# A hand-scheduled attention and two-MLP kernel: the written order of all steps is replaced by another order

## The chip, the cores and the metric

The kernel runs on one core of a Trainium2 chip. The metric is the device time of one execution in microseconds (us), as a median of several runs. Smaller is better.

## The reference

Three stages follow each other.

- Attention for 4 batches and 8 heads, with 576 positions and head size 64: scores are scaled, every score below the row's maximum minus tau is masked out, softmax is taken over the rest, and the result multiplies V.
- The first MLP on 2304 tokens of width 512: `h = x @ w_in` (512 to 2048), then a rational function of h elementwise (`g = P(h) / (Q(h) + 1e-6)`, a cubic over a quadratic in |h|), then `g @ w_out` back to 512.
- The second MLP: `a = x @ w1`, `b = x @ w2` (both 512 to 1024), `h = a * b @ w3`, and `h @ w_out2` to 512 columns.

Inputs and outputs are float32; the weights come as 64-bit floating point words.

## The kernel before

**Precision and weights.** Products that need it are made with a value split into a high and a low float16 part, three matrix products for one. The weights arrive as 64-bit words, 512 KB for a tile of 128 rows and 512 columns. `raw_w` (L670) loads one such tile into one of three buffers `wr`; `conv_w` turns it into a 32-bit tile `cw` in two steps (a cast on a chosen engine, L336 or L340, and a combination on VectorE, L681); `split_w` makes the high and low parts, partly with a small matrix product (L733, L734). `w_product` (L930) multiplies w3 by w_out2 once, so that the second MLP has one product less for each token. `norm_w` (L697) is a matrix product that sums squares of weights.

**Attention.** For each batch b, pair of heads c and block of 128 rows: `load_qk` and `load_v` fetch inputs; `scale_q` (L338 or L342) scales q by a factor that depends on tau (`limits`, L408 to L411, loads tau and makes this `flag`); `qk` (L507, L512) makes scores in the two banks `S` of PSUM; `top` (L521) takes row maxima; `thr`, `exp` (L541 to L548), `recip`, `p_norm`, `p_hi`, `p_lo` make normalized probabilities split in two; `p_t` (L584) transposes them by DMA into `pT`; `pv` (L599) multiplies by V; `x_split` and `x_tail` store the result in two parts `xp` and `xl`.

**MLPs.** The 18 token tiles n go through `h_product` (L809) for four chunks f, `act_h` (L817 to L824, ScalarE), `num` (L829, L831, VectorE, which ends the use of the bank of h), `den`, `inv`, `quotient` (L848 to L852 and a product L352), `turn` (L861, a transposing DMA from `gg` to `gt`) and `y_product` (L873). `y_norm`, `y_split` and another `turn` lead to the second MLP: `ab_product` (L980), `a_copy`, `c_mul` (L992 and two more), `turn`, `o_product` (L1009), `o_store` (L1021, L1025).

**PSUM.** There are two banks each (with places 0 and 1) of the tags `S`, `h` and `y`; `S` tiles are two banks wide. `h_product`, `pv`, `norm_w`, `w_product`, `scale_f` and most `ab_product` share the two places of `h`, so each must wait until the last reader of the place's former content is done.

**What sets the order.** All work is a list of 2533 events, numbered from 0. A text, `ORDER`, lists 3944 steps: each token is an event's number, and an event that has several steps stands several times. A letter behind the number says on which engine the step's free choice falls: `a` ScalarE, `v` VectorE, `p` GpSimd. Figures behind dots say which buffer or bank of a tag each new tile takes, in the order in which the step asks for tiles. The program is issued in exactly this order, so each engine, and SyncE (which issues all DMAs), works through its own steps in this order and waits at each for its inputs and for its buffer. Nothing else in the file decides the order. The events that the prediction speaks of are 1 (`limits`), 0 (`setup`: memsets on GpSimd, table load on ScalarE), 14 and 15 (`load_qk` and `scale_q` of the first q), 23 and 51 (the first two `qk`), 28, 36, 48 and 52 (`raw_w`), 30, 50 and 54 (`conv_w`), 56 (the first `w_product`), 80 (the first `pv`), 358 (`pv` of batch 0, pair 0, rows 256 to 511), 459, 478 and 527 (`h_product` of tile 0, chunks 1 and 2, and of tile 1, chunk 0), 2502 and 2503 (`o_product` and `o_store` of tile 15), 2531 and 2532 (the last `o_product` and `o_store` of tile 17).

The loop that issues the steps is this:

```
for token in ORDER.split():
    token, *where = token.split(".")
    places[:] = map(int, where)
    n = int(token.rstrip("apv"))
    eng[0] = token[len(str(n)):]
    if n not in gens:
        fn, args, *_ = events[n]
        gens[n] = fn(*args)
    if gens[n] is not None:
        next(gens[n], None)
```

Of the kernel before, what the change touches and what calls it, by code (L numbers as in the profile page):

```python
# [32 lines left out]
52.0 48.1 14.0.1 0 54p.0 54.0 50v.1 28.2 50.1 36.0 1 15a 23.0.1 30p.0 3 30.2 44.1 8.0 6.1 4.2  # L33
38a.1 10.2 25.0 27 29v.0 31.0.2 31v 33.3 33v 51.0.1 19.4.5 5.0.0 9.1 46p.0 46.3 7.0 35p 16.1 35
37p 45v.6 38.4 11.1 47 53.1 55 57v.1 59.1.7 62.8 21v 86.0.1 59a 12 12.0 12 18a.0 84v.0.0 84 32.0
13a.1.1 62a 64p 90.0.1 49.0 18.5 20.1 64 74a.3 13 76 92.2 24.2 88a 34v.1 39p.6 41p 94 22v.0
17a.2.2 22.6 96a.2 98.2.8 100.2 56.1 34.7 100a 17 66a 2 78 98a 102p 40.1 26v.0 43.1 119.0.1 26.8
68p.3 121.3 123 70p 56 102 113v.4 125a.0 115 127.3.5 61.0 63v.1 63.9 42v.0 42.10 127a 72 154.7.6
129.2 80.0.0 129a 158.1.0 131p 131 65.2 133v 82v 67v.1 103.0 104a 107p.3 82 109v 56 69.0 141a.8
160.0 56 69 162 117.0 75.1 105v.0 143 111.1 145 164p.1 105.11 166.4.4 168.2 166v 77p.0 67.12 168v  # L40
170v 116.0 186.1.0 77.13 106.2 135a.3 69 137v 170 172v 174p.8 188.1 152a.3.3 152 156a 190 176v
118p.1 69 58a.14 71a.15 79.1 118.16 192v.2 195.5.5 195a 139 81v.0 83.1 73.0 81.17 180v.0 83 182
108p.1 197.1 197a 108.18 147.0 199v 120.0 621.1 223.1.0 149a 149 132.2 122v.0 122.19 89.0 178.2
225.2 110.0 199 83 227 229p.0 231.6.4 231a 233.3 83 233a 235a 85a.20 91p.1 134v.0 110 134.21 136.1
201v 91.22 203p.2 205p 209a.8 211 184.0 252.1.0 110 110 97.1 624v.0 97 624.23 171.2 93.0 207 647.1
254.3 256 235 237a 258p.1 246a.0 260.7.6 260a 95v.1 95.24 97 97 248 641.0 219.7.5 650v.0 650.25
173p.1 262.1 645a.0 645.26 262a 221a 288 112v.27 124.1 290.1.0 291.0 264a 173.28 240a.2 652.0 242p
652 126v.0 163.0 264 126.29 274a.3 99a.30 213 266p 148.2 165a.1 293 150p.0 295a.2 165.31 140.1
150.32 652 628.0 297.0.4 276 613.1 298.8 298a 613 630p.1 297a 142v.0 314.0.1 142.33 316.1 300a
87.0 318 319a.0 613 300 321.1.1 321a 309v.5 128.0 630.34 250.1 613 616a.35 339.0 302v 304p.0 210.2  # L50
268p.7 212p.0 179.1 181a.1 278 155.0 311 284.8.3 286p 212.36 218.2 181.37 305v 633.1 220p.1 341.2
633 633 157a.0 633 157.38 342v.1 323.4 187.1 636v.39 270v 323a 652 655v.40 215.1 220.41 217a 217
130.0 60.0 159.0 138 194.0 167.1 161.1 226.2 196a.0 325v 169 175.0 344.2.6 189v.1 189.42 234.1 177
196.43 228v.1 144.1 325 146 183.0 228.44 202.0 185 185 151.1 241.2 153 153 312.0 191.0 193.1
204v.0 236p.1 344a 367.1.0 236.45 244.2 198.1 346v 327.1 346 659.0 114.0 200 204.46 230.0 243v.1
243.47 369.3 370 222.1 272 285.0 224.0 365 214.1 232 206.0 208 238.0 216 216 245.1 372a.2 239 326v
# [12 lines left out]
428v 380.0 407p 409 470p 470 478.0 357v.0 478 289.0 480.0 484.0.1 471p 480.0 661.1 480.0 392p.1
324.1 361.2 345.1 485p 482 479a.4 486.3 488 482 458 392.34 487 487 490p.0 454.0 491.7.8 690.0  # L70
493.3 472v 474p.2 491a 481 394.1 527.0 364a.1 661 357.3 359.1 724.1 489.0 493a 414 338.1 693p.0
364.10 366.1 678v.25 310.1 489 439.2 495a 509.0 511.0 396 281.0 281a 283.1 283a 396.1 396 424v.21
427v.41 455.1.0 401a.32 496.1 489 512a.1 527 406v.33 495 672v.29 417v.31 476p 514.0.7 399v.1 489v
514a 496 456p 417.0 516p 401.1 529.1 693.37 529.1 529.1 413a.38 534p 430.6 540.1.0 727p.1 492.1
499.0 440.1.0 499.0 417v 497a 401a 531 431v.28 408v.43 413.0 403a.42 531 432.0 498a.5 542.1 544
676v.46 546p.2 433v 403.1 413v 536 516 775.0 424.0 500p 403a 431.1 777v.0 473.2 501 420a.44 433
536 777.36 504a.6 477.1 434v.45 431a 727.47 499.0 503p 424a 547.1.8 549.2 435.0 549a 547a 505
664p.0 437a 506 422v.6 518a 434.1 501 427.0 712.2 545.1 434v 672.1 506 502 538.0 538 545 538 538v
695.1 442.0 672v 408.1 686a.12 415v.22 437 483.0 427v 698.0 701.1 551v 704p.0 507 410a.26 565.0.1
704.3 519v.3 436a.23 422.0 567.2 539 521p 569 444.1 570p.0 408a 449.1 429v.11 715a.1 715.10 415.1  # L80
# [1159 lines left out]
```

## Time and profile before

| | |
|---|---|
| median of three runs | 1026.38 us (1025.14 to 1026.40) |
| profiled execution, its own time | 1025.45 us |
| its span, first to last instruction | 1023.6 us |
| TensorE (PE) busy | 961.6 us, 94% |
| VectorE (DVE) busy | 799.8 us, 78% |
| ScalarE (ACT) busy | 673.8 us, 66% |
| GpSimd (POOL) busy | 337.0 us, 33% |
| mean granted clock of TensorE, share of full | 0.986 |

The own time of the profiled execution is 1.85 us more than its span: what lies around the first and the last instruction. Busy shares are means over the whole span; the rows further down tell them for stretches of it. SPq is SyncE's sequencer, which issues the DMAs.

### The profile page before, as it was taken

To read this page: it belongs to the slowest core of one execution; us is meant where nothing else is said; L and a number is where in the kernel's file an instruction comes from. 1 tells how busy PE (TensorE), PEld (TensorE's weight loads), DVE (VectorE), ACT (ScalarE), POOL (GpSimd) and SP (SyncE) were. 2 spreads that over 40 slices of the span, in tenths; PEclk is the share of its full clock that TensorE was granted. 3 is DMA by queue.
4 is the path that set the end of the run, shared out by engine and by line. 5 is a ranking of instruction groups with operands and counts; after the bars stand their busy time and mean duration, and the time that the engine had idled before them with its cause. 6 is when DMAs were issued, how large, how long until landed. Compare 5 with 4: busy or idle time off the path is not lost. (4 is left out here: it accounts for less than half of the span.)

```text
span 1023.6 us, 15533 instructions
## 1 busy us (share of the span) xinstructions
PE 961.6 (94%) x5260; PEld 459.4 (45%) x5260; DVE 799.8 (78%) x1529; ACT 673.8 (66%) x1262; POOL 337.0 (33%) x374
## 2 busy tenths in 40 slices
PE   2899787999899999999999999999999999999998
PEld 1344243444444444554545454544444444444443
DVE  5775699989798888998778788998888667676721
ACT  4546689998768897678667777787656435544411
POOL 2223134343233343532334333343233222233220
PEclk9999798999999999999999999999999999999999
DMA  8999879978857687957765685677664455333233
GB/s 285 230 235 251 244 211 216 212 200 194 187 124 147 140 150 169 201 130 151 148 135 117 135 181 115 151 134 150 125 130 91 97 107 104 70 60 69 60 58 76
DMA packets 334047, 153.32 MB, mean 150 GB/s; under 512 B 307344, under 2 KB 311440, under 8 KB 333968
## 3 DMA queue, kind: packets, MB, share of 16 engines
q1 hardware_dynamic: 333968, 152.34, 67.5%
q8 instruction: 41, 0.67, 0.3%
q14 instruction: 38, 0.31, 0.1%
HBM read 68.67 MB, written 8.13 MB: 75 GB/s over the span
## 5 line engine op out<-in xcount | busy, mean ns | idle before, releaser
L873 PE MATMUL y<-wp,gt 128*128 128x512 f16 x864 | 199.1, 379 | 0.7 <-DMA gt<-gg 0.5
L809 PE MATMUL h<-wp,xp 128*128 128x512 f16 x768 | 181.1, 384 | 11.5 <-DVE U L831 5.8
L980 PE MATMUL h<-wp,yy 128*128 128x512 f16 x576 | 131.7, 379 | 3.1 <-DMA yy<-d_y 1.2
L873 PEld LDWEIGHTS <-gt 128*128 128x128 f16 x864 | 82.7, 98 | 104.8 <-issue 7.1
L809 PEld LDWEIGHTS <-xp 128*128 128x128 f16 x768 | 74.3, 99 | 105.6 <-issue 17.4
L521 DVE TENSOR_REDUCE m<-S 128x1 f32<-128x576 f32 x144 | 103.8, 747 | 16.9 <-PE S L512 11.0
L352 POOL TENSOR_TENSOR gg<-A,r 128x512 f16<-128x512 f32 x45 | 61.5, 1368 | 161.2 <-DVE A L852 80.1
L512 PE MATMUL S<-raw 64*128 64x288 f32 x512 | 90.3, 452 | 21.5 <-ACT raw L338 14.1
L543 ACT ACTIVATE S<-S,th 128x576 f32<-128x576 f32 x125 | 86.8, 708 | 31.2 <-POOL th L359 15.8
L1009 PE MATMUL y<-wp,gt 128*128 128x512 f16 x432 | 101.0, 379 | 0.0
L548 ACT ACTIVATE p<-S,xy 128x576 f32<-128x576 f32 x125 | 92.3, 740 | 10.1 <-DVE hl L352 2.9
L980 PEld LDWEIGHTS <-yy 128*128 128x128 f16 x624 | 59.9, 98 | 79.1 <-issue 8.2
L352 POOL TENSOR_TENSOR A<-A,r 128x512 f32<-128x512 f32 x47 | 61.8, 1315 | 86.3 <-ACT r L824 81.4
L352 POOL TENSOR_TENSOR hl<-p,hl 128x576 f16<-128x576 f32 x50 | 66.8, 1337 | 58.1 <-ACT hl L336 28.2
L817 ACT ACTIVATE U<-h,cf 128x512 f32<-128x512 f32 x72 | 55.7, 774 | 42.7 <-PE h L809 34.0
L512 PEld LDWEIGHTS S<-raw 64*128 64x128 f32 x512 | 50.0, 196 | 59.0 <-issue 16.0
L848 DVE SCALAR_TENSOR_TENSOR gg<-U,cf,r 128x512 f16<-128x512 f32 x72 | 55.9, 777 | 25.7 <-ACT r L841 17.4
L839 ACT ACTIVATE r<-A,lnb 128x512 f32<-128x512 f32 x72 | 51.7, 718 | 36.8 <-POOL A L352 19.0
L829 DVE SCALAR_TENSOR_TENSOR U<-h,cf,U 128x512 f32<-128x512 f32 x72 | 53.5, 744 | 23.4 <-ACT U L817 12.6
L681 DVE SCALAR_TENSOR_TENSOR cw<-rw,head 128x512 int32<-128x512 int32 x72 | 51.8, 725 | 17.8 <-POOL head L340 10.7
L1009 PEld LDWEIGHTS <-gt 128*128 128x128 f16 x432 | 41.4, 98 | 51.1 <-issue 2.7
L349 DVE SCALAR_TENSOR_TENSOR hl<-p,su,hl 128x576 f16<-128x576 f32 x64 | 58.6, 919 | 4.5 <-ACT hl L338 4.1
(202 smaller groups left out, 1648.3 us busy)
## 6 DMA issues: line engine op xcount, KB each, us to landing
rw<-in_moe_w_dram SPq DMA_DIRECT2D x32, 511.8 KB, 4.4
rw<-in_moe_w_out_dram SPq DMA_DIRECT2D x24, 511.8 KB, 4.9
raw<-in_k_dram SPq DMA_DIRECT2D x32, 288.0 KB, 3.4
rw<-in_moe_w_in_dram SPq DMA_DIRECT2D x16, 511.8 KB, 5.0
wr<-in_v_dram SPq DMA_DIRECT2D x13, 576.0 KB, 4.6
out_dram<-A SPq DMA_DIRECT2D x16, 256.0 KB, 2.3
wr<-in_v_dram SPq DMA_DIRECT2D x12, 320.0 KB, 3.5
d_y<-x SPq DMA_DIRECT2D x13, 256.0 KB, 2.3
```

The lines of the kernel that those rows point to most:

```text
L349: nc.vector.scalar_tensor_tensor(o, x, scale, hi, op0=ALU.mult, op1=ALU.subtract)
L352: (nc.gpsimd if eng[0] == "p" else nc.vector).tensor_tensor(o, x, y, op=op)
L512: nc.tensor.matmul(t[s][:, half, :HS], x[r, o:o + 128], y[r, keys], start=True, stop=True)
L521: nc.vector.tensor_reduce(st["m", b, c, blk][:, s:s + 1], t[:, :, :HS], axis=AX.XY, op=ALU.max, negate=True)
L543: nc.scalar.activation(t, t, AF.Prelu, bias=th, alpha=BIG)
L548: nc.scalar.activation(x, t, AF.Exp, bias=xy[:, 0:1], accum_out=su)
L809: nc.tensor.matmul(t, x[:, y, c, o:o + 128], w[:, a, :], start=c + i == 0, stop=c == KD - 1 and i == 2)
L817: nc.scalar.activation(u, h, AF.Identity, bias=cf[:, 15:16], scale=cf[:, 0:1])
L848: stt(p[:, 0, :], u, cf[:, 3:4], r, ALU.add, ALU.mult)
L873: nc.tensor.matmul(st["y", n], x[:, 4 * a + j, :], w[:, y, :], start=f + j + i == 0, stop=f == 3 and j == 3 and i == 2)
L980: nc.tensor.matmul(t, x[:, 4 * y + c, :], w[:, a, :], start=c + i == 0, stop=c == KD - 1 and i == 2)
L1009: nc.tensor.matmul(st["o", n], x[:, 4 * a + j, :], w[:, y, :], start=hf + j + i == 0, stop=hf == 1 and j == 3 and i == 2)
```

## The change

`ORDER` is replaced by another list of the same 3944 steps of the same events. No function changes. The new order was found by a search that drew durations of VectorE, GpSimd and of landing transfers at random around their medians; the old one was found with the medians alone. Steps have moved by 8 places in the median; 148 stand at the same place. 580 steps run on another engine than before; the letters in all are `a` 479, `v` 379, `p` 323 before, and 496, 389 and 296 after. Many tiles take another buffer. The diff replaces all 250 lines; these are the ones around the steps named above.

```
-52.0 48.1 14.0.1 0 54p.0 54.0 50v.1 28.2 50.1 36.0 1 15a 23.0.1 30p.0 3 30.2 44.1 8.0 6.1 4.2
-38a.1 10.2 25.0 27 29v.0 31.0.2 31v 33.3 33v 51.0.1 19.4.5 5.0.0 9.1 46p.0 46.3 7.0 35p 16.1 35
...
-129.2 80.0.0 129a 158.1.0 131p 131 65.2 133v 82v 67v.1 103.0 104a 107p.3 82 109v 56 69.0 141a.8
...
-275v.19 332 350.5 450 416.0 459.1 445 387.1 381p.1 459 358.1.0 418.1 375.1 419a.1 421.5.8 421a
...
-428v 380.0 407p 409 470p 470 478.0 357v.0 478 289.0 480.0 484.0.1 471p 480.0 661.1 480.0 392p.1
...
-493.3 472v 474p.2 491a 481 394.1 527.0 364a.1 661 357.3 359.1 724.1 489.0 493a 414 338.1 693p.0
...
-2524.2 2496.0 2528a.0 2529 2496 2529p.1 2502 2525.1 2529v 2525 2530.0 2531 2531 2532a.1 2532 2502
-2503v.0 2503
...
+28.0 14.0.1 1 15p 52.1 8.0 0 30v.0 30.0 54v.1 23.0.1 25.0 36.2 27 54.1 29a.0 31.0.2 33.3 31v 33v
+35v 35 48.0 45v.4 50a.0 38p.1 38.2 47 4.1 5.0.0 50.3 9.1 51.0.1 3 10.1 11.0 53.1 55 6.2 7.1 57a.1
...
+42.8 26.9 72 75.2 119.0.1 56.1 113a.0 80.0.0 17 115 121.3 63a.1 65.1 104a 107v.4 109p 123 63.10
...
+441 267a 263.1 281v.24 363v 294a.0 294.22 87.1 387.0 347.1 261a 398v 358.1.1 402p 443.0 350v.1
...
+418.1 419p.1 421.6.7 421a 336.14 390.2 338.0 368.1 275v.19 269.1 452.0 360 273v.6 459.0 375.0
...
+308v.0 428p 467.5.4 471 308.23 354.1 478.0 471 471v 343.2 469.1 478 467a 331.1 469a 279a.5 484.0.1
...
+396 676a.20 669a.30 409 511.0 489 512p.1 493a 454.1 527.1 439.2 514.7.6 396.0 281a 474v.5 283v 396
...
+2521 2526.1 2526 2500v.1 2495.1 2527 2500p 2522v.0 2523 2523a.0 2523v 2496.1 2482.0 2482 2527 2488
+2488 2447 2501.0 2528a.1 2524.2 2529 2529v.1 2496 2489a.0 2502 2489 2529p 2519 2530.1 2502 2503a.1
+2525.0 2503 2525 2531 2531 2532a.0 2532
```

## Rows read from the trace of the kernel before

**Rows 1.** Busy time of each engine in stretches (instructions in brackets), TensorE's granted clock, DMA share

```profile
0.00:61.20 61.20, 37.52 (x118) 17.46 (x118) 41.12 (x89) 30.66 (x59) 16.92 (x29) 1.00 0.91 254
61.20:102.00 40.80, 38.43 (x135) 18.05 (x136) 26.34 (x46) 21.50 (x46) 11.54 (x14) 1.00 0.99 243
102.00:205.00 103.00, 84.16 (x402) 38.16 (x400) 89.64 (x183) 88.60 (x185) 35.10 (x39) 0.87 0.89 221
205.00:1000.00 795.00, 782.38 (x4520) 377.25 (x4521) 638.55 (x1208) 530.39 (x971) 272.83 (x293) 1.00 0.63 130
1000.00:1023.60 23.60, 19.13 (x89) 8.48 (x87) 4.17 (x6) 2.69 (x4) 0.61 (x1) 0.98 0.26 61
```

**Rows 2.** What TensorE waited for, 0 to 102: us in total, times, longest

```profile
PE S L512 <- ACT raw L338: 14.1, 2, 12.2
...
PE h L599 <- DMA pT<-hl: 2.0, 2, 1.7
PE h L930 <- DVE cw L681: 1.4, 1, 1.4
```

**Rows 3.** What TensorE waited for, 102 to 205

```profile
PE h L697 <- ACT sq L688: 4.6, 7, 1.3
PE h L809 <- DVE U L831: 4.5, 1, 4.5
PE h L809 <- DVE xp L349: 3.2, 1, 3.2
```

**Rows 4.** What TensorE waited for, 205 to 1000, longest and shortest of 17 rows

```profile
PE h L809 <- DVE xp L349: 1.5, 1, 1.5
...
PE h L809 <- DVE xl L349: 0.2, 1, 0.2
```

**Rows 5.** Timeline of all engines, 0 to 13: start, us, engine, line, operation, idle before

```profile
1.64 0.43 SPq L451 DMA_DIRECT2D raw<-in_q_dram  x1
...
2.59 3.64 SPq L670 DMA_DIRECT2D rw<-in_moe_w_out_dram  x2
4.38 0.76 POOL L340 CAST head<-rw 128x512 f16<-128x512 bf16 x1 [2.48 <-DMA rw<-in_moe_w_dram]
...
5.78 0.45 DVE L340 CAST head<-rw 128x512 f16<-128x512 bf16 x1
6.26 0.43 SPq L408 DMA_DIRECT2D tau_t<-in_tau_dram  x1
...
11.46 0.15 DVE L409 TENSOR_SCALAR flag<-tau_t 128x1 f32<-128x1 f32 x1 [4.50 <-DMA tau_t<-in_tau_dram]
```

**Rows 6.** Groups of instructions by shape: count, busy us, mean ns, idle before

```profile
L342 POOL TENSOR_SCALAR raw<-raw,flag 128x256 f32<-128x256 f32 x1 | 1.4, 1450 | 0.0
```

**Rows 7.** Timeline of TensorE, 10 to 64

```profile
29.75 2.07 PE L930 MATMUL h<-cw 128*128 128x512 f32 x2
...
42.38 1.17 PE L599 MATMUL h<-pT,vh 128*64 128x256 f16 x18 [1.68 <-DMA pT<-hl]
...
45.20 7.33 PE L930 MATMUL h<-cw 128*128 128x512 f32 x16
```

**Rows 8.** Timeline of TensorE, 95 to 210

```profile
142.75 2.75 PE L809 MATMUL h<-wp,xp 128*128 128x512 f16 x12
...
165.35 4.45 PE L809 MATMUL h<-wp,xp 128*128 128x512 f16 x12 [3.16 <-DVE xp L349]
```

**Rows 9.** Busy time in a stretch of ten us, columns as in rows 1

```profile
170.00:180.00 10.00, 5.48 (x20) 2.75 (x19) 8.64 (x17) 9.91 (x24) 5.62 (x7) 0.66 0.77 177
```

**Rows 10.** Timeline of all engines, 171 to 176

```profile
171.06 0.76 ACT L817 ACTIVATE U<-h,cf 128x512 f32<-128x512 f32 x1
...
175.01 0.74 DVE L831 SCALAR_TENSOR_TENSOR U<-U,cf,h 128x512 f32<-128x512 f32 x1
```

**Rows 11.** Timeline of all engines, 1007 to the end

```profile
1018.58 1.12 SPq L1025 DMA_DIRECT2D out_dram<-A  x2
...
1019.94 0.40 SPq L1021 DMA_DIRECT2D out_dram<-A  x1
```

More of the change, by code (lines that the diff above doesn't have):

```diff
@@ L45 @@
[L45 to L56, printed above, removed]
@@ new lines @@
+694.1 797.8 797a 795a 1146 928v.47 1199a.0 1152.1 719v 928 1152 615 719 680 1199v 1149.0 1202.2
+1149 720v 730a.4 931v.39 1155v.1 1157 737.0.1 723a.2 725p 728.2 1157a.1 740.0 742 1168.0 1207.1
+1157v 1160.0 931 733 1207 745a.0 747.0.5 749.7 749a 747a 799v 751a 1213a.1 799 802v 1168 1174
+1174v.0 780.1.2 819.1.0 751 754v 756a.0 821.1 1210.1 824 759v 811a.6 762 614.0 1174v 1177.1 814
+1210 1216 697a.1.1 614 935 782a 825a.1 828.1.5 831.8 828a 831a 689.0.1 935 816.0 608 1188 1216p.1
+691v 618.0 618.0 691 862.0.1 648.1 618.0 864.2 764a.0 648 1216p 734.1 833a 867 833 1163.1 1163
@@ new lines @@
+882.1 1073.0.0 891p 958 940.0 940.0 887 887 1401.1 959.0 1075.1 874 940.0 1009.2 946p 972a 896
+1401 896 949 949 943 1081.2 943 1011 973p.5 1012a.0 1014.5.4 960.0 975v 976 900.0 981 952.1 900
+1014a 900 1015.7 983.1 952 1006 984.3 952 1015a 952v 960 1017a 986p.1 954.0 900v 904.1 1017
+1405a.1 1025v.2 1003.8.1 1026 1403.1 1403 987.7.5 963.0 987a 989p 989 963.0 990v 1407 963.0 1019a
+968p 992a.0 874 971 1028.2 994p 965 1020p.7 1030.0.1 971 1031.0 1033 1034a.2 965 1036.0.6 974.1
+1037.5 1037a 974 957.0 957 982.1 982 974 974v 909 995.2 1036a 1039p 909 1407v.0 1407p 1039 1410.2
@@ new lines @@
+1018v 1421 1136.0 1120a 1137a.0 1062p 1139.6.3 1041 926 1043.1 999.1 1111.1 1043.1 1139v 1043.1
+1104p 1087v 1140v 1122v 1421p.1 1421p 1122 1140 1129a.0 1226.2 1064.5 1046 1161 1435.0 1435
+1439a.0 1433 1076.0 1046 1131 1162.1.0 1002 1002 1164.1 1021.0 1165 1084 1142a 1123a 1049p 1052
+1620.1 1065.0 1052 1423.1 1167v.1 1169.4.7 1125v.4 1126v 1169a 1170.5 1054.0 1069.1 1106.0 1054
+1054 1024 1054p 1170a 1024 1184.1.0 1133 1172a 1144p.6 1172 1173a 1145p 1067v 1128 1067 1070v
+1027.0.1 1027 1029a 1437.0 1412 1437 1186.2 1187 1057.0 1189p.2 1179a.8 1181 1190.7.2 1070 1063.1
@@ new lines @@
+1063 1190a 1442 1175v.0 1176p 1442p.0 1147.3 1029 1192.5 1192a 1193a 1442p 1066.1 1084.0 1206.1
+1084 1552.2 1208.3 1066.0 1209v.0 1066.0 1621.1.1 1465.3 1071p 1349a.2.2 1193 1195a 1449.0 1552
+1449 1552 1197v.4 1426 1032.0 1426 1453a.0 1158.6.7 1159a 1068 1198p 1068 1349 1211.5.1 1211a
+1178.2 1201v.0 1074 1212p 1212 765 1151.0 1074 1077.1 1398 1077 1228a.0.0 1148.1 1150a 1150
+1233.0.1 1214a 1215a.2 1444.2 1077 1153a 1060.0 1153 1038 1287.1 1183.0 1428a.1 1235.0 1200 1237
+1077p 1085.1 1217p 1218.3 1203 1239a.1 1085 1088.1 1204 1241.0.8 1446.1 1088.0 1088.1 1093p
@@ new lines @@
+1320 1285v 1323.0 1340 1335v 1337 1323 1323 1361.3.7 1363.5 1363a 1361a 1365a 1365 1285 1742.0
+1282 1323p 1284.0 1379.1.0 1286 1381.1 1383 1284.0 1284.0 1384a.0 1286 1342 1386.4.1 1386a
+1351.6.2 1243 1388.0 1035 1352p 1746.0 1288p 1325.0 1746 1141 1261 1261 1388a 1390a 1390 1344.1
+1367v 1462 1345v 1751 1751a.1 1760.0 1399a.4 1368p.8 1345 1291 1411.1.0 1742 1291 1413.2 1415
+1370p 1372.1 1751v 1374v.3 1376 1400 1753.2 1293.0 1293 1293 1263.0 1293p 1263 1266.1 1266.1
+1266.1 1268 1416a.1 1268 1418.5.7 1418a 1420.8 1420a 1765.1 1765 1769v.0 1270p 1272 1272 1377.0
@@ new lines @@
+1452p 1477.0.5 1478.7 1478a 1309 1138 1353 1477a 1467 1785p.1 1966 1346 1353 1464.1.8 1785v 1788.1
+1469.1 1359.0 1469.1 1359 1359 1359v 1469.0 1480p 1366.1 1366 1369.0 1474v 1476 1480 1482p
+1494.1.0 1369.0 1362.2 1472 1472 1552 1371 1454 1776.1 1476 1456v.4 1457 1369.1 1373p 1375 1404.0
+1496.1 1371 1434.0 1364 1498 1484v.2 1500a.1 1375 1776 1406v 1406 1790 1378.1 1964.1 1378 1378
+1459 1501.1.6 1501a 1378p 1790 1519.1 1521.2 1503.0 1503a 1523a.2 1505v 1524.2.3 1505 1466v
+1514a.4 1546 1524v 1526v 1486p 1487.1 1479.0 1504.1 1504 1506.0 1479 1526 1364 1489a.5 1506.0 1491
@@ new lines @@
+1506.1 1511v 1513 1969.0 1479 1509 1969 1547.0.1 1973a.1 1479p 1549.3 1528a 1530a.7 1461.0 1380.0
+1531p 1509 1493.0 1551 1794.1 1481.1 1463v 1463 1507a 1516 1553a.0 1513 1533.2 1515.1 1515 1762
+1515 1554.6.3 1517 1556.0 1971.1 1556a 1971 1792v.1 1554a 1485.0 1485 1558a 1792 1508p.5 1552
+1488.0 1572.1.0 1382 1515p 1975 1975v.0 1522.1 1382 1518.2 1574.0 1510p 1488.0 1576 1558 1488.0
+1492p 1495 1495 1522 1490 1490 1535.0 1567v.8 1560v 1561p.6 1975v 1563p 1568 1542.7.4 1577a.1
+1483.1 1483 1544v 1537v.0 1537 1525.1 1497.1 1497 1497 1525.1 1497p 1982.0 1982 1579.3.2 1579a
@@ new lines @@
+1996a.1 1601 1996 1612.0 1615 1683 1601 1603.1 2003.1 1704.6 1731a 1612.1 1603 1612.1 1603 1615
+1747.0.1 1733v 1855.0 1617p 1619 1619 1748.2 1750 1603p 2033 1733 2003 1622.0 2007a.1 1605.1
+1752v.1 1622 1754.1.3 2005.0 1754a 2005 1756.4 2017.1 2010 1734a 1796v.3.3 2017 1717.7.8 1796 1622
+1771.0 1608 1773.3 1659.0 1659 1736a.1 2021v.0 1775v.2 1713.1 2033 1738p 2010a.1 1917a.0.0
+1777.6.5 1777a 2010v 1718a 1778a 1741v.2 1622v 1917 2012.0 1661.1 1608 1624.2 1706.1 1663 1756a
+1757a 1661.0 1757 1801.0.1 1661.0 1743 1759v 1778 1803.0 1780a 1665p 1761a.6 1663 1708v 2014.0
@@ new lines @@
+1782p.0 1668 1805 1708 1668 1784v 1626 1670.1 1740.2 1763v 1626 1766v.1 1807a.0 1629.3.0 1629
+1786.5 1764 1670 1670 1809.3.3 1631a 1670p 1768 1710.0 1809a 1640.1 1745.0 1631 1711a 1711 2001
+1715v.1.1 1810.0 1810a 1715 1812a 2014 1640 1812 1642.1 1642.1 1642.1 2019.0 1647p 1649 1635 2019
+1814a 1645 2023 1826.0.1 1633.1 1787.0 1770 2023p.0 2023p 1645 1828.1 1638 1821a.4 1789a 1830
+1832a.2 1789 1791.1 1793a 1677.0 1649 1823 1833.5.6 1835.2 1835a 1672.1 1793 1652.1 1652 1695.1
+1833a 2026.2 1837v 1837 1839v 1652 1798.1.7 1800a 1677 1550 1695 1679.0 1679.0 1679.0 1825.1
@@ new lines @@
+1831.0 1922.1.0 2243 1831 2030a.1 1897 1899a 1901a.8 1903p 1906v.2 1908 1811.0 1881a.5 1834.1
+1707v 1709.1 1834.0 1834.1 1924.0 1926 1928p.2 1905 1883 1857 1929.0.0 1931.6 1929v 1931v 1850.1
+1836 2243p.1 1850 1838p 1840 1836 1840 2243p 1843.0 1933a 1933 1843 1843 1852.0 1693 1843p 1854
+1885.0 1919.8.5 1920a 1910 1947.1.0 1949.1 1935a 1936p.1 1813.0 1813 1815.1 1811 1951 1952a.1
+1954.2.7 1818 1693 1712 1712 1938p 1854 1954v 1818 2030 1852.0 1956.2 1845.0 1956v 1852.0 1958p
+1979.1.0 1958 1981.2 2253.1 1815.1 1815.1 1820p 1856p 1983 1714.1.0 2245.2 1822 1714 1822 1824.1
@@ new lines @@
+2185a 2098 2139p 2139 2123.0 2114.0 2097 2400v.0 2158 2399.1 2199.0.1 2114 2114 2114v 2097 2187p
+2404.0 2201.3 2307 2203 2204a.0 2206.1.0 2206a 2399 2207.4 2222.0 2116.2 2207a 2401 2401p.0 2404
+2119 2141a 2209p 2512.1 2512 2160p 2161a.1 2163v 2393.0 2119 2223.0 2147a.6 2225p.2 2149 2187
+2164.7 2122.3.1 2227.3.8 2188a 2190v.1 2122 2191p 2124a 2195a.2 2227v 2124 2401v 2127.3 2513
+2132.1 2132 2209 2135.1 2138 2138 2135.1 2150 2196 2211p 2388.0 2135.0 2506.0 2506 2142a.3 2144v
+2145 2140v 2402.2 2507 2513 2507 2405.1 2405 2514v.0 2515 2172.6.5 2388 2515a.1 2515v 2212a.3
```

394 lines of the change are left out of this document (169 added, 225 removed).

## The prediction

> **What bounds the kernel now.** I read first the table of busy time by stretches [rows 1], then the list of what TensorE waited for in each stretch [rows 2 to 4], and last the timelines at the places that this list points to [rows 5, 7, 8, 10, 11]. The table shows three parts. From 205 to 1000 TensorE is busy 782.38 of 795.00 us, so an order can win at most 12.6 us there. From 102 to 205 it is busy 84.16 of 103.00, so 18.8 us are idle, and its granted clock is 0.87; but VectorE is busy 89.64 and ScalarE 88.60 of the same 103, so here three engines share the limit. From 0 to 61.2 it is busy 37.52, and 23.7 us are idle, 12.2 of them ahead of the first score product [rows 1, 2]. From 61.2 to 102 only 2.4 us are idle. The products themselves don't change, so the time can move only through these idle stretches, through the products that ran at the low clock, and through the last 4.5 us after 1000 [rows 1].
>
> **The start.** The first score product waits 12.2 us for the scaled q [rows 2], and the scaling waits for tau: VectorE makes `flag` at 11.46, as soon as tau has landed [rows 5]. In the old order SyncE comes to tau only at 6.26, since it stands behind four weight loads, and the fourth needs a buffer: the issue of the third and fourth reaches from 2.59 to 6.23 [rows 5]. In the new order only one weight load, q and k stand ahead of tau. The first weight tile of 512 KB had landed by 4.38, when its cast began; the second was cast 1.40 us later, at 5.78 [rows 5]. At that pace q and k (128 and 288 KB) take 1.1 us, so tau could be there at 5.5. The other bound is the time from tau's issue to its use, 11.46 - 6.26 = 5.2 us: issued as fourth with 0.43 us each, at about 2.0, it is there at 7.2. I take 6.5, nearer the middle, because the 5.2 contain the traffic of more loads than will stand ahead of it. Behind it come `flag` (0.15 us, [rows 5]) and the scaling, which now falls on GpSimd: 1.45 us in the one row of that shape [rows 6]. So the first product starts at about 8.2 instead of 12.2: -4.0 us, between -5.0 and -3.2. The heads' memsets now stand behind this scaling on GpSimd, and the first two casts on VectorE wait for them, ahead of the first row maxima; at less than 3 us in all that delay hits VectorE before it has maxima to take, and I leave it inside the next term's bounds.
>
> What becomes of these 4.0 us is decided at the first `pv`, which started at 42.38 after a wait of 1.68 us for the transposed probabilities [rows 7]. Two things change here. First, the new order brings `pv` forward, ahead of the second step of the first `w_product`; four products of 0.46 us, from 7.33 us for 16, are 1.8 us [rows 7] that formerly filled the wait and now follow it. Second, the chain that ends in this transpose has less ahead of it: adding up the steps that precede the last `p_hi` in both orders, each at the mean duration of its kind on its engine in this trace, I find VectorE 21.9 and 21.3 us, ScalarE 18.3 and 14.5, GpSimd 10.3 and 5.1. So the chain should move forward with the start and about 1 us more. Sum for the start: -4.0 + 1.8 - 0.8 = -3.0. Bounds: +1.8 if the chain is held by something that does not move with tau (transfers: DMA share 0.91 up to 61.2 [rows 1]), and -5.0 if the lighter ScalarE and GpSimd queues count in full.
>
> The price of those four products depends on the clock, and here a row and a page can be held together. In the row at 29.75 two products of this shape took 2.07 us, at 45.20 sixteen took 7.33 [rows 7]: 1.03 and 0.46 us each, the two levels of 1.2 and 2.4 GHz, although the granted clock of the stretch reads 1.00 [rows 1]. The Trainium skill, "TensorE: Matmul & The Clock Gate", section on the HAM clock gate, says that the low level is the default and that activity releases it. By that rule a TensorE with less to do before the first `pv` may stay low beyond it; what that would cost is the third rival below.
>
> **102 to 205.** Two waits lead the list beside the squares of weights: 4.5 us for VectorE L831 and 3.2 us for VectorE L349, both ahead of `h_product` [rows 3]. The first is event 527, which takes the bank of event 478 when only 1.6 us of TensorE work lie between them (summed with mean durations over the steps between). The bank becomes free only after `act_h` and `num`: from 171.06 to 175.75, 4.7 us [rows 10]. In the new order 527 takes another place whose last user, `scale_f`, is 3.3 us of products away, and two pieces of `split_w` were put ahead of it. That wait can go: -4.5. With it could go the low clock that followed: the ten us from 170 show a granted clock of 0.66 after TensorE had stood idle [rows 9], and twelve products at 165.35 took 4.45 us where twelve at 142.75 took 2.75 [rows 8], 1.7 us more; two such groups make -3. On the other side VectorE and ScalarE are the limit as well. Counted between the same two points of TensorE's work (77 and 160 us of it), the new order has 103.9 us of VectorE work for 105.4, and 107.7 us of ScalarE work for 104.1. If ScalarE carries the end, this is +3.6. I take -2.0, between -7.5 and +3.6: nearer the engines' limit, since a wait that goes at one place comes back at the next while VectorE is full.
>
> **205 to 1000.** Seventeen rows from 1.5 down to 0.2 us make up the 12.6 us [rows 4]. For each kind of chain from TensorE back to TensorE I summed the products that lie between its ends. Where a place is taken over from an `h_product`, the least cover was 1.6, then 3.9 us; in the new order it is 5.2. From `ab_product` to `o_product` the least was 6.6, now 7.9; from `h_product` to `y_product` 13.1, now 15.8. The mean covers hardly change (9.0 and 9.0, 10.0 and 11.0, 14 and 14 in whole us for `quotient` to `y_product`). So the thinnest places were thickened, not all. VectorE gets 5.0 us more work over the whole kernel, ScalarE 5.6 more and GpSimd 19 less; VectorE is busy 638.55 of 795.00 [rows 1], so that is covered by its idle time. I take -2.0 (a sixth of the 12.6), between -6 (half) and +6 (as many new ones as half the old).
>
> **The end.** The old order ends with `o_product` and `o_store` of tile 15, one store, issued in 0.40 us; the new one ends with tile 17, two stores issued in 1.12 us [rows 11]. Everything else being equal, +0.6 (0.72 less the difference of the scaling's engine).
>
> **Sum.** -3.0 - 2.0 - 2.0 + 0.6 = -6.4. Against the profiled execution's own 1025.45 (span 1023.6 and 1.85 around it; 0.9 below the median of the runs) that is 1019.05; I say 1019.0.
>
> **The rivals.**
>
> First, nothing that counts: the start is gained, and given back before 205 because VectorE and ScalarE set the pace there. For it speaks that they are busy 87% and 86% of that stretch [rows 1] and that their work does not shrink. Against it: up to 102 VectorE is busy only 67.5 of 102 us [rows 1], so the work ahead of the stretch can move forward with the start. Then -3.0 + 3.0 - 0.5 + 0.6, about 1025.5, and 1024.3 to 1028.4 as a case. Chance 0.14.
>
> Second, slower, through one bank. In the new order event 478 takes over the place of 459, another `h_product`, with 5.6 us of products between; before, it took the place of `pv` 358 with the same 5.6 and still waited 3.2 us [rows 3]. An `h_product`'s place needs three ScalarE and two VectorE instructions to be freed, 4.7 us when VectorE was as full as there [rows 10], a `pv`'s place only the two steps of `x_split`. Each us beyond 5.6 is a us of TensorE, and the low clock behind it costs 1.7 for twelve products [rows 8]. The chain must be 5 us later than its cover, with two such groups behind it, to eat up the 6.4 and more: then +2 to +8, about 1030, and 1028.4 to 1034 as a case. Against it: VectorE gets 1.5 us less there. Chance 0.15.
>
> Third, TensorE stays at the low level longer at the start. If eight more `w_product` pieces behind the first `pv` run at 1.03 instead of 0.46 us [rows 7], that is +4.6, and if the transposes are not earlier either, the start gives +1.8 + 4.6 instead of -3.0: 1028.4 to 1030. By the rule named above this could happen; that the matmuls at 45.20, right behind the `pv`, ran at the high level [rows 7] speaks against it. Chance 0.05.
>
> Fourth, all terms near their good ends: -4.5 - 6 - 4 + 0.6, below 1012. Chance 0.06.
>
> My forecast, 1012 to 1024.3, has 0.60. A measurement of this kernel can tell about 0.2%, 2.05 us, from no change. So faster by more than that: 0.60 + 0.06 = 0.66; within it 0.14; slower 0.15 + 0.05 = 0.20. The range from 1011 to 1030 leaves out some 0.05 below and 0.12 above.
>
> **What would show it.** In the changed kernel's profile the first L512 product should start between 7 and 9 us, and the first L599 before 40. The waits of L809 for L831 between 102 and 205 should fall under 2 us, and the granted clock of 160 to 180 should be near 1. From 205 on the idle time should be below 12. The prediction is wrong if the stretch between the same points of work (norms of weights to the last `split_w` of w_out) takes longer than before, which its VectorE and ScalarE shares would show at 9 tenths or more, or if a single wait of more than 3 us stands behind 205.

## The result, and the profile after

The changed kernel takes 1012.8 us in the median of four runs (1011.54 to 1015.13), the kernel before 1026.39 (1025.14 to 1027.14). The ratio is 0.9871, 95% interval 0.9849 to 0.9894: 13.2 us faster, 11 to 15.5. The profiled execution is the slowest of the four: own time 1015.13, span 1013.3. Against the profiled execution before (1025.45) that is -10.3 us, and the sums below account for these.

Busy time by stretches in the kernel after (columns as in [rows 1]):

```profile
0.00:61.20 61.20, 29.60 (x97) 14.61 (x98) 39.32 (x82) 26.10 (x49) 11.82 (x20) 1.00 0.80 239
61.20:102.00 40.80, 40.36 (x143) 18.39 (x142) 30.23 (x55) 20.39 (x46) 13.20 (x15) 1.00 0.94 236
102.00:205.00 103.00, 89.12 (x411) 42.03 (x410) 83.25 (x181) 94.18 (x194) 35.84 (x47) 0.87 0.91 225
205.00:1000.00 795.00, 789.21 (x4577) 382.14 (x4576) 635.18 (x1229) 539.91 (x987) 258.73 (x267) 1.00 0.64 132
1000.00:1013.30 13.30, 8.12 (x38) 3.49 (x36) 0.00 (x0) 1.38 (x2) 0.08 (x1) 0.93 0.41 99
```

Up to 61.2 us TensorE did 7.9 us less than before (29.60 for 37.52): the start was lost, not won. From 102 to 205 it did 5.0 us more, with ScalarE at 94.18 of 103. Behind 205 it stands idle for 5.8 us instead of 12.6. The waits of TensorE in the kernel after, for 0 to 102, then 102 to 205, then 205 to 1000, answer to [rows 2 to 4]:

```profile
PE S L512 <- POOL c L399: 10.4, 1, 10.4
PE h L477 <- DVE vs L474: 6.7, 1, 6.7
PE S L512 <- ACT p L548: 6.6, 3, 5.1
PE S L512 <- ACT raw L338: 4.4, 1, 4.4
...
PE h L697 <- ACT sq L688: 3.2, 6, 1.6
PE S L507 <- issue: 2.6, 1, 2.6
...
PE h L980 <- DVE U L831: 2.3, 2, 1.4
PE h L980 <- DMA yy<-d_y: 1.9, 1, 1.9
PE h L599 <- DVE xp L349: 0.4, 1, 0.4
```

Both waits of `h_product` (L809) that stand in [rows 3] are gone from the middle list. Behind 205 six rows remain of seventeen. The first row names a memset; what the product waited for is the scaling of q in front of it on GpSimd, as the timeline further down shows.

Stretches of equal time mix places once two kernels have drifted apart. So I also compare **at equal work**: each TensorE instruction is weighed with what it takes at the high clock (0.216 us for a 512-column float16 product, for example), and I look when the sum reaches a value. Time of the kernel after minus the kernel before, in the two profiled executions:

| us of TensorE work done | 1 | 5 | 40 | 60 | 95 | 160 | 200 | 250 | 500 | 750 | end |
|---|---|---|---|---|---|---|---|---|---|---|---|
| time before | 14.5 | 35.3 | 75.4 | 97.7 | 151.0 | 231.2 | 273.8 | 326.0 | 582.7 | 841.3 | 1019.1 |
| after, difference | -1.8 | +10.5 | +7.8 | +5.8 | +0.6 | +1.6 | 0.0 | +0.2 | -4.3 | -10.8 | -11.0 |

The first score product is 1.8 us earlier, but by 5 us of work the new order is 10.5 us behind. All of that is regained by 200, and in these two executions all of the gain arises between 250 and 750 (326 to 841 us of the kernel before). Behind the last product lie 5.2 us instead of 4.5, so +0.7. One profile is not exact to better than 2 to 3 us here: three other kernels below whose first 1067 steps are those of the new order are at +6.2, +6.7 and +7.0 at 40, and at -2.7, -1.7 and -0.4 at 200. Four other kernels that begin with the old order stand at about +2.1, +1.3, -0.1 and +2.7 at 200. On average the two beginnings are thus some 2.4 us apart there, for the new order: most of the gain lies further back, but not quite all.

### The profile page after: what moved, and what is told of

Its sections match the earlier page's. It is cut to its first block, busy times and chain, and to the rows that moved or that the text cites. A ratio compares the mean times of both kernels' runs of the same rounds, so it can differ in the third digit from the quotient of the medians.

```text
span 1013.3 us, 15519 instructions
## 1 busy us (share of the span) xinstructions
PE 956.4 (94%) x5260; PEld 460.6 (45%) x5260; DVE 788.0 (78%) x1545; ACT 682.0 (67%) x1274; POOL 319.7 (32%) x347
## 4 chain that ended last, share of the span: by engine, by line
PE 84%; DMA 6%; DVE 4%; ACT 3%; issue 2%; POOL 1%; SPq 0%; ACTq 0%; POOLq 0%; DVEq 0%
PE y L873 17%; PE h L809 17%; PE h L980 12%; PE y L1009 9%; PE S L512 6%; PE S L980 6%; PE h L599 5%; PE h L930 5%; PE y L733 3%; PE S L507 2%; DMA rw<-in_moe_w_out_dram 1%; DMA rw<-in_moe_w_in_dram 1%; DMA x<-gg 1%; DMA pT<-in_v_dram 1%; PE y L734 1%
## 5 line engine op out<-in xcount | busy, mean ns | idle before, releaser
L809 PE MATMUL h<-wp,xp 128*128 128x512 f16 x768 | 178.1, 380 | 0.2 <-ACT r L824 0.2
L809 PEld LDWEIGHTS <-xp 128*128 128x128 f16 x768 | 73.7, 98 | 93.7 <-issue 8.6
L352 POOL TENSOR_TENSOR gg<-A,r 128x512 f16<-128x512 f32 x38 | 50.7, 1334 | 167.9 <-DVE A L852 112.4
L352 POOL TENSOR_TENSOR hl<-p,hl 128x576 f16<-128x576 f32 x53 | 71.1, 1343 | 93.1 <-ACT hl L336 43.8
L543 ACT ACTIVATE S<-S,th 128x576 f32<-128x576 f32 x119 | 82.5, 708 | 26.6 <-DVE th L359 13.6
L548 ACT ACTIVATE p<-S,xy 128x576 f32<-128x576 f32 x119 | 87.9, 741 | 3.5 <-DMA pL<-hl 0.7
L352 POOL TENSOR_TENSOR A<-A,r 128x512 f32<-128x512 f32 x45 | 58.2, 1293 | 90.8 <-ACT r L824 89.3
L848 DVE SCALAR_TENSOR_TENSOR gg<-U,cf,r 128x512 f16<-128x512 f32 x72 | 57.8, 804 | 15.3 <-ACT r L841 9.4
L821 ACT ACTIVATE A<-h,cf 128x512 f32<-128x512 f32 x72 | 49.1, 683 | 16.4 <-DVE U L831 9.5
```

Source lines behind the costliest of these rows:

```text
L352: (nc.gpsimd if eng[0] == "p" else nc.vector).tensor_tensor(o, x, y, op=op)
L543: nc.scalar.activation(t, t, AF.Prelu, bias=th, alpha=BIG)
L548: nc.scalar.activation(x, t, AF.Exp, bias=xy[:, 0:1], accum_out=su)
L809: nc.tensor.matmul(t, x[:, y, c, o:o + 128], w[:, a, :], start=c + i == 0, stop=c == KD - 1 and i == 2)
L848: stt(p[:, 0, :], u, cf[:, 3:4], r, ALU.add, ALU.mult)
```

## The experiments

Each kernel was timed beside the kernel before on the same chip, and one execution of it was profiled. Where a kernel's own list of steps has more lines, the line numbers in its rows are 5 to 8 higher.

**Where in the order the gain lies.** Two splices: the first steps of one order, then the steps of the other that were not yet done, in that one's sequence. Some 45 tiles needed another buffer, and each splice has a price of its own at the seam.

```
old_then_new:  first 921 steps of the old order (to about 233 us), then the new one
new_then_old:  first 1067 steps of the new order (to about 262 us), then the old one
```

> The old order for its first 921 steps, up to about 233 us of the old trace, then the remaining steps in the new order; 43 buffer places are renumbered where the cut needs it. Theory late (the whole gain comes from waits of TensorE behind 270 us, and the first part of the new order is a draw): 1011 to 1016 us. Theory early (as the prediction split it, about half of the gain or more lies ahead of 205 us): 1018 to 1022 us.

> The mirror image: the new order for its first 1067 steps, up to about 262 us of the old trace, then the remaining steps in the old order; 46 buffer places renumbered. Theory late: 1024 to 1029 us. Theory early: 1017 to 1021 us.

Measured: old_then_new 1020.45 us (ratio 0.9946, 0.9927 to 0.9964), new_then_old 1028.49 (1.0032, 1.0020 to 1.0044). At equal work old_then_new is 5.8 us behind the kernel before at 250, right behind the seam, and 4.0 ahead at the end: it gains 9.8 us in the new order's later part. new_then_old is 3.8 behind at 250 and 5.1 behind at the end: with the new order's first part alone nothing is gained later. So most of the gain belongs to the sequence behind 250 us of work. The totals alone would not show it: that of old_then_new lies in the range of theory early, since the seams cost 4 to 6 us.

**Sequence or engines.** The old sequence with its buffers, but with the engine letters of the new order:

```
-52.0 48.1 14.0.1 0 54p.0 54.0 50v.1 28.2 50.1 36.0 1 15a 23.0.1 30p.0 3 30.2 44.1 8.0 6.1 4.2
+52.0 48.1 14.0.1 0 54v.0 54.0 50a.1 28.2 50.1 36.0 1 15p 23.0.1 30v.0 3 30.2 44.1 8.0 6.1 4.2
...
```

> The old sequence of steps and the old buffers, with only the engine letters of the new order. Theory sequence (the gain comes from where steps stand between TensorE's products): 1024 to 1034 us, no faster than before and perhaps slower, since letters and sequence no longer fit each other. Theory letters (the gain comes from 19 us less on GpSimd and the new split of work): 1013 to 1019 us.

Measured: 1141.47 us, ratio 1.1127 (1.1108 to 1.1146), far above what either theory gave. It loses all along: 17 us by 95 of work, 44 by 250, 115 at the end. The waits that lead its list (lines 7 higher):

```profile
PE S L519 <- POOL raw L349: 15.5, 3, 13.4
PE h L816 <- DVE U L838: 13.0, 8, 4.0
PE h L816 <- DVE xp L356: 9.0, 3, 5.6
```

The letters alone do not carry the gain: the engines are busy about as long as in the kernel after (VectorE 809.7 us for 788.0, ScalarE 682.2 for 682.0, GpSimd 320.0 for 319.7), and the time is 129 us more. A letter is good only with the places around it. The opposite exchange, the new sequence with the old letters, was not run.

**The lost start.** The rows of the kernel after, timeline of all engines, 0 to 13, answer to [rows 5, 6]; behind them the third and fourth rows of TensorE, and the rows of ScalarE ahead of them:

```profile
2.12 0.43 SPq L408 DMA_DIRECT2D tau_t<-in_tau_dram  x1
...
9.20 0.15 DVE L409 TENSOR_SCALAR flag<-tau_t 128x1 f32<-128x1 f32 x1 [9.20 <-DMA tau_t<-in_tau_dram]
...
9.45 0.93 POOL L342 TENSOR_SCALAR raw<-raw,flag 128x256 f32<-128x256 f32 x1 [9.03 <-DVE flag L409]
...
10.44 2.29 PE L512 MATMUL S<-raw 64*128 64x288 f32 x8 [10.44 <-POOL c L399]
...
11.09 0.73 DVE L340 CAST head<-rw 128x512 f16<-128x512 bf16 x1 [1.49 <-POOL head L404]
...
12.57 0.33 SPq L670 DMA_DIRECT2D rw<-in_moe_w_dram  x1
...
25.86 0.56 PE L477 MATMUL h<-vs,c 128*128 128x1 f32 x2 [6.68 <-DVE vs L474]
30.81 1.32 PE L512 MATMUL S<-raw 64*128 64x288 f32 x2 [4.39 <-ACT raw L338]
...
27.02 1.26 ACT L338 ACTIVATE vh<-pT,vs 128x1152 f16<-128x1152 f32 x1 [1.31 <-DVE vs L441]
...
30.26 0.50 ACT L338 ACTIVATE raw<-raw,flag 128x256 f32<-128x256 f32 x1
```

tau is issued 4.1 us earlier than before, but lands 7.1 us after its issue instead of 5.2. Behind it stand the memsets, the first cast (11.09 instead of 4.38) and with it the next weight load (12.57), behind which SyncE holds three of the four loads of V. Two repairs:

```
new_setup_first
-28.0 14.0.1 1 15p 52.1 8.0 0 30v.0 30.0 54v.1
+28.0 14.0.1 0 30v.0 30.0 1 15p 52.1 8.0 54v.1
new_loads_early
-25.0 36.2 27 54.1 ... 3 10.1 11.0 ... 6.2 7.1 ... 44.2 19.5.6 12
+25.0 36.2 10.1 6.2 19.5.6 27 54.1 ... 3 11.0 ... 7.1 ... 44.2 12
```

> The new order with one repair of its start: the memsets of setup and the first conv_w stand ahead of limits, so they no longer queue behind tau on GpSimd and VectorE, and the weight loads, which stood still from 3.97 to 12.57 us for a buffer, can go on at about 6 us. The first score product should still start at about 10.4. Theory absorbed (VectorE and ScalarE, full from 100 to 200 us, swallow a lead as they swallowed the deficit of 6 to 10 us that the new order had at its start): 1010.5 to 1013.5 us, the same as the new order within 2 us. Theory carried on (what the start loses or gains reaches the end): 1004 to 1008 us.

> The new order, with two load_v (events 10 and 6) and the load_qk of the next pair (event 19) issued right behind the third weight load, ahead of the weight load that waited for its buffer until 12.57 us; no place or letter changes. If the new order's lost start comes from these loads standing behind a waiting issue, scale_v moves from 25.9 to 21 to 23 us, the third score product from 30.8 to 25 to 28, and the deficit at 5 us of TensorE work against the kernel before falls from 10.5 to 6 or less. If it comes from something else, the deficit stays at 9 or more. In both cases the stretch up to 205 us takes the difference up, and the total is that of the new order within 2 us: 1011 to 1015.

Measured: new_setup_first 1011.55 us (0.9863, 0.9850 to 0.9877), new_loads_early 1010.02 (0.9828, 0.9807 to 0.9850). In the first, the deficit stays: 9.6 us at 5 of work, 7.8 at 40. In the second it is 9.0 and 5.5, and `scale_v` and the third score product move by 1.6 us only. Rows of new_loads_early (SyncE, ScalarE, then TensorE):

```profile
14.60 0.33 SPq L461 DMA_DIRECT2D wr<-in_v_dram  x1
...
19.57 0.74 ACT L468 ACTIVATE jk<-wr 128x640 bf16<-128x640 f32 x1 [0.58 <-DMA wr<-in_v_dram]
...
24.27 0.56 PE L477 MATMUL h<-vs,c 128*128 128x1 f32 x2 [5.33 <-DVE vs L474]
29.22 1.32 PE L512 MATMUL S<-raw 64*128 64x288 f32 x2 [4.40 <-ACT raw L338]
```

So the memsets did not hold the start. The loads were tested in part only: in both repairs one load of V (event 4) was still issued only at 14.41 and 14.60 us (14.84 in the change as given), and ScalarE's squares of V, for which `scale_v` waits, begin with it (19.57 above). What the rows show besides is ScalarE's sequence: the third score product waits for `scale_q` on ScalarE (30.26 above), which is issued behind the `vh` step that waits for `scale_v`, a cast and two softmax steps, while the old order scaled this q on VectorE, at 22.53. The Trainium skill, "TensorE: Matmul & The Clock Gate", section "Architectural detail: the array is 16× 32×32, not 1× 128×128", says that the queues of ScalarE and VectorE are worked off strictly in order; the rows agree, since this scaling starts only when the instructions issued ahead of it are done. An order with this one letter changed was not run, so the cause of the deficit stays open. Of the kernels that leave nothing out, new_loads_early is the fastest: 2.8 us below the change as given by the medians, where at most 2 were expected, but the two intervals just touch.

**What a lost start costs at the end.** The old order's first 150 steps, then the new order:

```
old_start_then_new:  ... 168.2 166v 77p.0 67.12 | 152a.3.3 152 77.13 116.1 ...   (27 tiles in other buffers)
```

> The first 150 steps (some 52 us of the time before) stand in the old order, all others in the new one; 27 tiles take another buffer. So the first score product starts near 12 again and the first pv near 42, while the new order's start was 7.8 us behind at 40 us of TensorE work. If the new order's lost start is taken up before 200 us of work anyway (absorbed), the old start buys nothing: 1011 to 1016 us, and the time at 200 us of work is within 2 us of both kernels. If the lost start is carried on to the end, the old start wins it back: 1003 to 1007 us, and the point of 200 us of work comes 6 us or more earlier.

Measured: 1013.79 us (0.9873, 0.9851 to 0.9895), the same as the change. The test is less clean than meant: at the seam a score product waits 5.6 us, so that this kernel too is 8.9 us behind at 40, in spite of its early start. But it is 1.2 behind at 95, 1.4 at 160 and 0.2 ahead at 200. Over all kernels of this study but that with exchanged letters, the differences at 40 reach from -0.3 to +8.9 us, and at 160 from -1.2 to +1.6. A deficit at the start is taken up, wherever it comes from.

**More cover by hand.** A wait of TensorE can be given cover by bringing later, independent steps ahead of it. Nine and three such moves in the old order, of this kind:

```
-859v 937 939.0.1 739 808 935 783 709.1 679 910
+859v 937 808 679 939.0.1 739 935 783 709.1 910
```

> The old order, in which nine TensorE steps that waited behind 270 us (qk 1,0,2; y_product 3; qk 1,2,3; ab_product 3; h_product 6; pv 2,0,1; pv 2,1,2; ab_product 7,1; h_product 11; together 6.8 us of waits) start 2.6 us of TensorE work later, because two later independent steps are brought ahead of each. No letter changes. If thin cover of single chains is what the old order lost behind 270 us, these waits go and don't come back: 1019 to 1021.5 us. If the waits show the pace of the engines behind TensorE, they turn up again at the next steps: 1024.5 to 1027 us.

> The old order with only three of the nine moves (qk 1,0,2; qk 1,2,3; h_product 6), those behind which the run with nine regained 1.0, 1.6 and 1.1 us at the place. If behind 270 us each us of wait that goes is a us of the end, and each new one too, the end comes 2 to 3.7 us earlier: 1022 to 1024.3. If the gains at single places are taken back by the engines behind, it is the time before: 1025 to 1027.

Measured: nine moves 1039.68 us (1.0129, 1.0110 to 1.0149), slower than either theory gave; three moves 1025.87 (0.9986, 0.9973 to 0.9999), so 1.4 us by the ratio where 2 to 3.7 were expected. At equal work, in steps of 6 us, the reason shows. With three moves 1.0, 1.6 and 1.1 us are won, each at its place, and 1.0 and 1.2 lost within 12 us behind the second, and the rest in smaller pieces: the profiled execution is 2.6 us behind the kernel before at 250 us of work and 2.9 at the end, so of the 3.7 nothing is left in it. With nine, new waits of up to 2.3 us arise where there were none or short ones; its list (lines 5 higher):

```profile
PE y L878 <- DMA gt<-gg: 3.1, 2, 2.3
PE h L814 <- DVE U L836: 2.3, 1, 2.3
PE h L604 <- DVE U L836: 2.3, 1, 2.3
PE y L1014 <- DMA gt<-gg: 1.7, 1, 1.7
```

The delayed step starts its own chain 2.6 us later, and the step brought ahead meets its input with 2.6 us less to spare. Cover is moved, not made. My first theory, that a few thin covers could be thickened one by one, falls.

**More and less VectorE work.** In both orders, for the tiles 2 to 11, the first VectorE instruction of `quotient` issued twice, or the third left out:

```
-        stt(p[:, 0, :], u, cf[:, 3:4], r, ALU.add, ALU.mult)
+        [stt(p[:, 0, :], u, cf[:, 3:4], r, ALU.add, ALU.mult) for _ in range(2 if 2 <= n < 12 else 1)]
...
-        stt(t, u, cf[:, 3:4], t, ALU.add, ALU.subtract)
+        2 <= n < 12 or stt(t, u, cf[:, 3:4], t, ALU.add, ALU.subtract)
```

> The old order with the first VectorE instruction of quotient issued twice for the tiles 2 to 11, 40 more instructions of 0.78 us, 31.1 us of VectorE between about 280 and 840 us; the results stay the same. If the new order's gain is greater tolerance of late chains, the old one loses clearly more by this than the new one: old 1034 to 1042, up 8 to 16. If the orders differ by a few accidental fits only, both lose the same, within 2 us.

> The new order with the same 40 VectorE instructions doubled. Tolerance: 1013 to 1018, up by 5 at most and by at least 4 less than the old order. Accidental fits: the same loss as the old order within 2 us, so 1021 to 1029.

> The old order with the third VectorE instruction of quotient left out for the tiles 2 to 11 (so the low half of g is not the reference's there): 40 instructions of 0.81 us less, 32.6 us of VectorE between about 280 and 840 us. If the old order's loss against the new one is margins too thin for the lateness of the chains, it gains most of its 12 us of idle time there: 1014 to 1019. If TensorE's own sequence sets its pace, 1022 or more.

> The new order with the same 40 instructions left out. Margins: it has little left to gain, 1007 to 1011, and the distance to the old order with the same cut is under 9 us, where it is 13 now and 18 with the doubled instruction. If the new order has another advantage than margins, the distance stays at 12 to 14.

Measured: doubled, old 1046.79 us (1.0198, 1.0181 to 1.0215) and new 1028.62 (1.0027, 1.0013 to 1.0041); left out, old 1023.24 (0.9965, 0.9951 to 0.9980) and new 1008.57 (0.9816, 0.9795 to 0.9838). By the ratios the two orders are 17.5 us apart with more VectorE work, 13.2 as given and 15.3 with less. The new order loses some 4 us less by the extra work than the old one, as tolerance wants, but 16 us instead of at most 5, and the old one 20 instead of 8 to 16. With less VectorE work the distance should have shrunk below 9, and did not. So lateness of VectorE alone is not what separates the orders.

To see what does, I counted in each profiled execution, between 250 and 750 us of work, the TensorE instructions that started over 0.15 us later than the median spacing of their kind and for which the trace names a releaser; and of the TensorE steps between 276 and 850 us those that had less than 0.3 us from their last input, landing or freed bank to their start:

| kernel | length, 250 to 750 | late starts | us in all | of these, released by VectorE | steps with under 0.3 us to spare |
|---|---|---|---|---|---|
| before | 515.3 | 21 | 12.1 | 8.1 | 48 of 261 |
| after | 504.3 | 3 | 3.0 | 2.7 | 25 of 265 |
| old_fast_vector | 509.7 | 14 | 7.2 | 2.4 | 38 of 262 |
| new_fast_vector | 501.0 | 1 | 0.4 | 0.4 | 23 of 267 |
| old_slow_vector | 535.7 | 37 | 30.2 | 21.4 | 62 of 252 |
| new_slow_vector | 522.9 | 25 | 18.0 | 11.9 | 52 of 257 |
| old_more_cover | 527.4 | 22 | 21.2 | 8.3 | 52 of 254 |
| new_loads_early | 503.3 | 3 | 2.8 | 2.6 | 24 of 266 |

9.1 of the 11.0 us between before and after are late starts that are gone. In the old order 8.1 us of them follow VectorE and 4.0 ScalarE, GpSimd and landings. Less VectorE work takes most of the first part away, and the rest stays (4.8 us in old_fast_vector, none in new_fast_vector). A second count of the same kind, which gives 12.0 and 3.3 us for the first two rows, finds 4.5 us of late starts in old_then_new and 13.6 in new_then_old; of steps with under 0.3 us to spare it finds 49 before, 21 after, 26 and 46. So the late starts go with the later sequence. The waits of TensorE from 326 us on, the four longest of nine rows in old_fast_vector, then new_fast_vector, where one row is all there is:

```profile
PE y L873 <- DMA gt<-gg: 1.1, 1, 1.1
PE S L512 <- ACT p L548: 0.7, 1, 0.7
PE h L599 <- DMA pL<-hl: 0.7, 1, 0.7
PE h L599 <- ACT U L338: 0.5, 1, 0.5
...
```

```profile
PE h L980 <- DVE xl L349: 0.3, 1, 0.3
```

## Why the prediction came out as it did

The sum was -6.4 us, and 1019.0; measured -10.3 in the profiled execution, and 1012.8 in the median, near the low end of the range. Two of its four terms lay outside their own bounds, in opposite directions. That the total fell into the stated range is in part luck: it holds because the error at the start did not reach the end, and the sum had not counted on that.

**The start: predicted -3.0 (between -5.0 and +1.8), measured +7.8 at 40 us of work.** Two steps failed. First, "tau could be there" by 5.5 to 7.2: it landed at 9.20, because a flight is not a constant; the 5.2 us of the kernel before were taken as an upper bound, and it was 7.1. The first product came at 10.44, not between 7 and 9. Second, and larger: "the chain should move forward with the start". I summed the work that stands ahead of the first `pv` on each engine, found less of it, and left the order in which SyncE and ScalarE come to it out; which of the two held it is not shown. The first `pv` came at 48.30, not before 40 (42.38 before).

**What becomes of it.** The first rival was right that what happens at the start is given back before 205, with the sign turned round: it expected a gain to be lost there; a loss was regained. That is why an error of 10 us in the first term did not reach the total. Its reason, that VectorE and ScalarE set the pace there, is not shown. At 102, 151 and 205 us of the kernel before, the kernel after is about 5.5, 1.3 and 1.8 us behind at equal work. So the loss was regained ahead of 151, where before VectorE was busy 79% and ScalarE 76%. From 151 to 205, where both were busy 95%, nothing came back. Two stretches before, then the first of them after:

```profile
102.00:151.00 49.00, 39.52 (x151) 17.25 (x150) 38.50 (x89) 37.16 (x75) 13.18 (x16) 0.83 0.82 229
151.00:205.00 54.00, 44.64 (x252) 20.92 (x250) 51.14 (x96) 51.44 (x110) 21.93 (x24) 0.91 0.96 215
...
102.00:151.00 49.00, 42.79 (x186) 20.66 (x185) 34.86 (x83) 41.66 (x83) 11.89 (x18) 0.86 0.97 250
```

The weight transfers are a rival here (DMA share 0.82 and 0.97), and no run separates them from the engines.

**102 to 205: predicted -2.0 (between -7.5 and +3.6), measured about -3.7 between these two times of the kernel before, and -7.8 from 40 to 200 us of work (75 to 274 us)** with the deficit ahead of it. The wait of 4.5 us for L831 is gone, and so is the one of 3.2 us, as expected; no wait of L809 stands in that list. But most of the 7.8 is the deficit taken up: kernels with the new order's first part end between 0.0 and -2.7 at 200, so what the stretch won beyond that is 0 to 3 us. The granted clock of the two stretches that I named was not near 1; before, they read 0.83 and 0.66:

```profile
160.00:170.00 10.00, 8.41 (x55) 3.87 (x55) 9.77 (x19) 9.94 (x23) 4.05 (x4) 0.83 0.58 160
170.00:180.00 10.00, 6.41 (x16) 2.40 (x16) 9.30 (x22) 9.94 (x24) 3.54 (x4) 0.76 0.88 196
```

ScalarE is busy 9.94 of 10 us in both, as it was before [rows 9]: TensorE still waits there, for other reasons. Between the points 77 and 160 of work that I named for a failure, the time fell from 110.3 to 106.4 us.

**205 to 1000: predicted -2.0 (between -6 and +6), measured -11.0 from 200 us of work to the end, and about -12.8 from 205 us on.** This is the step that decided. The mechanism named, thin places made thicker, holds in the counts above; its size was read from the wrong quantities. I compared the least and the mean covers in TensorE work, found the mean unchanged, and took a sixth of the 12.6 us. The mean to spare is indeed nearly unchanged (median 1.5 before, 1.7 after), but it is the thin end that waits, and there the count was halved, from 48 to 25. And the 12.6 us of listed waits were not the whole sum: from 326 to 841 us the list holds 8.6 us, while late starts, by the spacing of the products, come to 12.1.

**The end: predicted +0.6, measured +0.7** (two stores issued in 1.13 us from 1008.92).

**The rivals.** The bank of event 478 cost nothing: no wait of L809 in the stretch. TensorE did not stay at the low level beyond the first `pv`; the rows of TensorE in the kernel after, as [rows 7]:

```profile
44.59 3.78 PE L930 MATMUL h<-cw 128*128 128x512 f32 x4
48.30 1.44 PE L599 MATMUL h<-pT,vh 128*64 128x256 f16 x18
49.57 0.71 PE L599 MATMUL h<-pT,vl 128*64 128x256 f16 x10
50.21 3.70 PE L930 MATMUL h<-cw 128*128 128x512 f32 x8
53.84 1.24 PE L512 MATMUL S<-raw 64*128 64x288 f32 x8
```

Four products took 3.78 us ahead of the first `pv`, eight took 3.70 behind it. All good ends together (below 1012) came closest to the measured time, but not by its own terms: its start was a loss.

**What stays open:** which instruction holds the new order's start, what takes its deficit up ahead of 151 us, and how much of the gain behind 250 belongs to which moves. The experiments show that it is the later sequence, that it is spread over many thin places and all releasers, and that single moves in the old order do not reach it.

## What to carry to other kernels

When an in-order schedule is replaced, count its thin end in the trace: how many steps of the bounding engine start less than a few tenths of a us behind their last input. Means and minima of cover say little, and the list of waits shows only part of the lateness. A deficit at the start can be taken up later: here 7.8 us at 40 us of work were 0.6 at 95. So price a change at the start by what is left further on, at equal work; that full helper engines do this is not shown here. Moving one step for more cover takes the cover from its neighbours: nine plausible moves cost 13.6 us, and three that had each paid at their place, 3.7 us together, brought 1.4 by the ratio.

## What the runs showed of the hardware

A load of 512 bytes in 128 packets of four took 7.1 us from issue to landing, with three larger loads issued behind it. DMA share and GB/s in 40 slices of 3 to 12 us in the kernel after, and the issue's row in the view of transfers:

```profile
DMA  9979999457112459767989988989989984100000
GB/s 382 441 269 414 293 383 358 144 114 67 69 59 83 91 128 146 182 237 291 419 314 389 446 369 369 469 362 446 441 364 455 384 330 168 57 20 41 18 18 36
...
tau_t<-in_tau_dram SPq DMA_DIRECT2D x1, 0.5 KB, 7.1
```

Between 5.2 and 5.7 us the share falls to a tenth, and the rate to 69 and 59 GB/s, while these packets are under way, and other loads had been issued. The Trainium skill, "DMA: Bandwidth & Descriptors", section Specifications, gives 512 bytes as the least transfer for full rate; the trace agrees in that the rate falls where the small packets are: of the 240 packets of four bytes that it lists up to 13 us, 151 start between 4.5 and 7.0. It gives each 7 to 9 ns, so what filled the rest of that time it does not show.

The low level of TensorE's clock shows in the durations (eight score products in 2.29 us at 10.44, in 1.24 at 53.84), while the granted clock of that stretch reads 1.00. And work on VectorE has no one price: 31.1 us more cost 20 us in the old order and 16 in the new, 32.6 us less brought 4 and 6, although VectorE was busy 76 to 80% of the span in all of them.
